# Softcap attention and a maxout MoE in one launch: left values in one pass, named score slots, larger weight loads, a new order of all work

## The chip, the cores and the metric

The kernel runs on one core of a Trainium2 chip. The core has a matrix engine (TensorE, PE in the profile, with its weight loads shown as PEld), VectorE (DVE), ScalarE (ACT), GpSimd (POOL) and SyncE (SP), each with its own list of instructions that it runs in order, and DMA queues that SP, ACT and POOL issue to. All matmuls here take bf16 operands and accumulate in float32 in PSUM. The metric is the device time of one launch in microseconds (us); a profile is of one execution, and its span is a little shorter than the time of that execution.

## The reference

```python
def _attn_ref(q, k, v, cap):                      # q, k, v: 8 x 12 x 448 x 64
    scale = 1.0 / np.sqrt(q.shape[-1])
    scores = scale * np.matmul(q, k.transpose(0, 1, 3, 2))
    scores = cap * np.tanh(scores / cap)          # cap = 30
    scores = scores - np.max(scores, axis=-1, keepdims=True)
    attn = np.exp(scores)
    attn = attn / (np.sum(attn, axis=-1, keepdims=True) + 1e-09)
    return np.matmul(attn, v)

def _moe_ref(x, w1, w2, w_out):                   # x: 3584 x 768
    g = np.maximum(x @ w1, x @ w2)                # w1, w2: 768 x 1024
    return g @ w_out                              # w_out: 1024 x 768

# x is the attention's output, (8, 448, 12 * 64) laid out as 3584 x 768
```

## The kernel before

**The algebra.** max(h1, h2) = relu(h1 - h2) + h2, so the kernel computes relu(x (w1 - w2)) w_out + x (w2 w_out). It makes w1 - w2 once (`subtract`, L377) and w2 w_out once (`turn_w2` L391 transposes w2, `premultiply` L406 multiplies, `keep_wm` L412 copies out). `stage1` is then x (w1 - w2) with a relu on the way out of PSUM (L627), `stage2` the two products summed in one PSUM bank, 6 + 8 matmuls, with a copy out (L660).

**The items.** The 96 heads are 24 items t of four heads, each item two pairs i = 2t + o. Keys stand in PSUM's rows, queries (448) in its columns. The 448 keys of a head are three blocks of 128 and a left block of 64. Per item:
- `scores` (L486): for each pair and each of three key blocks, two heads side by side as 64x128 tiles, into one slot of two banks; `tanh` (L491) on ACT empties it into the exps' tile. There are two such slots, taken in turn by scores, left scores and values alike.
- `left` (L499): the left 64 keys of all four heads, four 64x64 tiles at once; `tanh_left` (L503).
- `ex` (L507) and `ex_left` (L510): exp in place, on ACT; no maximum is subtracted, since tanh bounds the scores.
- `add` (L519) and `add_left` (L524) sum the exps of the key blocks on DVE, from item 3 on; `total` (L537, L541, L544) sums over the keys by a matmul with ones; `invert` (L549, L552, L555) takes 1/x on DVE.
- `values` (L569): 128x32 tiles, four heads abreast, three passes for the 128-key blocks, for each half u of the 64 value columns; then the left keys by one more pass of 128x32 (L573), in which half of the rows of the weights (`vl`) are zeros, since the left exps of two heads lie above each other. `fill_const` (L287, L288) writes the zeros once. `normalize` (L582) multiplies by 1/sum into `xT`, the x of the MoE, one DVE instruction per u.

**The MoE** works on groups: one PSUM bank, its matmuls and its way out. `Group.step` (L606) issues half a matmul (64 rows of the contraction, 64x128 tiles), and `M x y n` does n steps of two groups x and y, one in the upper and one in the lower half of the array; with -1 for one of them, half of the array is empty. Where x = y, step 2 issues full 128-row matmuls (L601); the last two groups run so. When a group moves from one half of the array to the other, `hand_over` (L615) puts a DVE nop between. Groups have one of four banks, `mm0` to `mm3`, which also serve totals and transposes.

**The loads.** `load` (L322, L329) and `load_v` (L347) bring q, k and v on POOL's queue, which casts to bf16. The first ten pairs (NX) are turned by PE (`transposes` L433, `keep_qkT` L441), later items by a DMA transpose on SP (`cross`, L453), which frees the raw tile `kqs`; k/q, v and the transposed tiles have two buffers each (KB, VB, QB). w2, w_out and w1 are loaded on POOL's queue too (L368, L359, L374): w1 and w2 in six blocks of 128 x 1024. Stores go out on SP (L637, L638, L642), those of the last tile on SP and ACT (L665 to L672). `keep_warm` (L449) issues filler matmuls early on.

**The order.** All of this is in one list of steps, ORDER, written out in the kernel and executed once to issue instructions: S scores, T tanh, L and TL left scores, E and EL exp, A and B adds, Y the total, V values, N normalize, O opens a group, M steps groups, H hands over, ev evicts, st stores, lk, lq, lv, lw1, lw2, lwo loads, cr a DMA transpose, X and XC a transpose by PE and its copy, W, P, OP, PC the premultiply, D fillers. Each engine runs its part of the list in that order and waits where data or a buffer is not there. MoE steps of the batches that are done fill PE between the attention steps of the next items; after item 23's values, PE has only MoE work. An excerpt, with item 4's values:

```python
M 10 8 3; L 5; Y 4 0; TL 5; V 4 0; Y1 4; V 4 1; E 10 0 3; Y2 4; Y3 4; S 11 0; M 10 9 1; lv 6 0; N 4 0;
M 10 9 2; M 8 9 1; N 4 1; M 8 9 1; lv 6 1; M 8 9 2; H 10; M 8 9 1; S 11 1; lv 6 2; T 11 0; A 5 0 1; M 8 9 3;
```

Of the kernel before, what the change touches and what calls it, by code (L numbers as in the profile page):

```python
# [9 lines left out]
ld0 k; ld0 q; ms0; lk 1 0; dm; ms; D 3 34; lw2 1; id; lq 1 0; lk 2 0; lw2 2;  # L10
cd k; cd q; lq 2 0; Xh 0 0 0; lwo 0 0; Xh 0 1; XCh 0 0; lw2 0; XCh 0 1;
lwo 0 1; S 0 0; lq 3 0; S 0 1; lq 4 0; T 0 0; lk 3 0; D 3 4; S 0 2; X 1 1; T 0 1; XC 1; D 3 6;
lv 0 0; W 2 2; T 0 2; W 1 3; lv 0 1; WC 2; L 0; E 0 0 3; S 1 0; WC 1; X 2 0; XC 2; D 3 8;
lv 0 2; OP 2 0 1; P 2 0 3; TL 0; P 2 0 1; OP 1 0 2; P 1 0 3; T 1 0; P 1 0 1; S 1 1; lv 0 3; W 0 3; EL 0; S 1 2;
WC 0; T 1 1; OP 0 0 0; P 0 0 2; T 1 2; P 0 0 1; S 2 0; lk 4 0; P 0 0 1; P 1 0 1; E 1 0 2; P 1 0 1; lw1 0;
S 2 1; P 1 0 2; P 2 0 1; lwo 1 0; P 2 0 1; PC 1 0; P 2 0 2; T 2 0; P 0 0 1; lk 5 0; PC 2 0; X 3 3; lw2 3;
E 1 2 3; P 0 0 1; XC 3; S 2 2; lwo 1 1; P 0 0 2; T 2 1; PC 0 0; lq 5 0; T 2 2; X 4 2; lq 6 0; L 1; lv 1 0;
XC 4; Y 0 1; TL 1; lv 1 1; sub 0 0; V 0 0; E 2 0 3; V 0 1; Y1 0; S 3 0; Y2 0; Y3 0; lv 1 2; OP 0 1 3; P 0 1 1;
T 3 0; N 0 0; P 0 1 3; lv 1 3; N 0 1; OP 2 1 0; P 2 1 2; EL 1; P 2 1 2; S 3 1; S 3 2; T 3 1; OP 1 1 2; P 1 1 2;
lw2 4; W 3 1; P 1 1 1; T 3 2; P 1 1 1; WC 3; S 4 0; E 3 0 2; S 4 1; OP 3 1 1; P 3 1 4; lw2 5; P 0 1 3; T 4 0;  # L20
P 0 1 1; P 1 1 1; lv 2 0; P 1 1 1; PC 0 1; P 1 1 2; E 3 2 3; P 2 1 1; lv 2 1; PC 1 1; S 4 2; X 5 3; lv 2 2;
T 4 1; P 2 1 1; XC 5; P 2 1 1; lv 2 3; P 2 1 1; T 4 2; OP 3 0 2; P 3 0 2; PC 2 1; lw1 4; L 2; Y 1 3; lk 6 0;
TL 2; V 1 0; lk 7 0; Y1 1; E 4 0 3; V 1 1; Y2 1; Y3 1; S 5 0; lq 7 0; N 1 0; W 5 0; lw1 2; W 4 3; N 1 1; T 5 0;
P 3 0 1; WC 5; P 3 0 1; lw1 5; S 5 1; EL 2; P 3 0 1; lw1 1; WC 4; S 5 2; P 3 0 1; lq 8 0; T 5 1; P 3 0 2;
P 3 1 2; PC 3 0; P 3 1 1; T 5 2; lk 8 0; P 3 1 1; OP 4 0 0; P 4 0 1; sub 4 0; P 4 0 3; lk 9 0; E 5 0 2; X 6 3;
PC 3 1; lq 9 0; P 4 0 2; XC 6; P 4 0 2; lw1 3; X 7 2; PC 4 0; S 6 0; XC 7; S 6 1; T 6 0; OP 5 0 1; P 5 0 2;
lv 3 0; sub 2 0; P 5 0 3; E 5 2 3; P 5 0 1; S 6 2; P 5 0 2; T 6 1; OP 4 1 3; P 4 1 1; lv 3 1; sub 5 0; P 4 1 4;
T 6 2; P 4 1 2; L 3; PC 5 0; Y 2 0; lv 3 2; TL 3; V 2 0; sub 1 1; Y1 2; E 6 0 3; V 2 1; Y2 2; Y3 2; S 7 0;
N 2 0; X 8 2; lv 3 3; N 2 1; X 9 1; T 7 0; lq 10 0; XC 8; P 4 1 1; EL 3; S 7 1; XC 9; S 7 2; lq 11 0; OP 5 1 0;
P 5 1 2; PC 4 1; P 5 1 1; T 7 1; P 5 1 1; A 3 0 1; P 5 1 2; lk 10 0; P 5 1 2; T 7 2; sub 3 0; O 0 2; M 0 -1 1;  # L30
lk 10 1; S 8 0; M 0 -1 1; E 7 0 2; M 0 -1 1; S 8 1; PC 5 1; lk 11 0; M 0 -1 2; A 3 0 2; M 0 -1 1; O 1 1;
M 1 -1 1; lk 11 1; M 1 -1 1; H 0; M 1 -1 1; T 8 0; M 1 0 1; A 3 1 1; M 1 0 1; lv 4 0; M 1 0 1; O 2 3; M 2 0 1;
B 3 0; M 2 0 1; E 7 2 3; lv 4 1; S 8 2; M 2 0 1; H 1; B 3 1; M 2 1 1; lv 4 2; M 2 1 1; T 8 1; M 2 1 1; ev 0;
O 3 0; M 3 1 1; lv 4 3; M 3 1 2; T 8 2; H 2; A 3 1 2; M 3 2 2; lk 12 0; cr 5; M 3 2 1; ev 1; O 4 2; M 4 2 1;
L 4; lk 12 1; M 4 2 1; TL 4; Y 3 1; V 3 0; lq 12 0; Y1 3; E 8 0 3; V 3 1; Y2 3; lk 13 0; Y3 3; S 9 0; M 4 2 1;
lv 5 0; N 3 0; M 4 3 2; N 3 1; M 4 3 1; lv 5 1; O 5 1; M 5 3 2; T 9 0; H 4; M 5 3 1; ev 2; lv 5 2; S 9 1;
M 5 4 1; ev 3; M 5 4 1; EL 4; M 5 4 1; lv 5 3; S 9 2; A 4 0 1; O 6 3; M 6 4 2; lk 13 1; M 6 4 1; T 9 1; H 5;
A 4 0 2; M 6 5 3; lq 13 0; ev 4; O 7 0; M 7 5 1; T 9 2; M 7 5 1; S 10 0; H 6; M 7 5 1; M 7 6 1; E 9 0 2;
lk 14 0; M 7 6 1; ev 5; S 10 1; M 7 6 1; O 8 2; M 8 6 1; lk 14 1; M 8 6 1; H 7; M 8 6 1; M 8 7 2; ev 6;
lq 14 0; T 10 0; M 8 7 1; O 9 1; M 9 7 1; A 4 1 1; M 9 7 2; E 9 2 3; lk 15 0; H 8; S 10 2; ev 7; M 9 8 3; cr 6;  # L40
B 4 0; lk 15 1; M 9 8 1; T 10 1; M 9 8 2; B 4 1; M 9 8 2; lq 15 0; T 10 2; M 9 8 2; A 4 1 2; M 9 8 1; O 10 3;
M 10 8 3; L 5; Y 4 0; TL 5; V 4 0; Y1 4; V 4 1; E 10 0 3; Y2 4; Y3 4; S 11 0; M 10 9 1; lv 6 0; N 4 0;
M 10 9 2; M 8 9 1; N 4 1; M 8 9 1; lv 6 1; M 8 9 2; H 10; M 8 9 1; S 11 1; lv 6 2; T 11 0; A 5 0 1; M 8 9 3;
lv 6 3; O 11 0; M 11 9 1; A 5 0 2; EL 5; M 11 9 1; S 11 2; M 11 9 1; lk 16 0; ev 8; M 11 10 2; T 11 1;
M 11 10 1; ev 9; M 11 10 1; cr 7; M 11 10 1; lk 16 1; M 11 10 2; T 11 2; M 11 10 1; S 12 0; lq 16 0; M 11 10 1;
# [12 lines left out]
M 20 18 2; L 7; lq 20 0; ev 18; Y 6 1; TL 7; V 6 0; Y1 6; lk 21 0; V 6 1; E 14 0 3; Y2 6; Y3 6; lk 21 1;
S 15 0; M 20 19 1; N 6 0; M 20 19 1; lv 8 0; M 20 19 1; N 6 1; O 21 0; M 21 19 2; lv 8 1; M 21 19 1; H 20;
S 15 1; T 15 0; ev 19; M 21 20 1; lv 8 2; M 21 20 2; A 7 0 1; O 22 1; M 22 20 1; EL 7; M 22 20 1; lv 8 3;  # L60
S 15 2; H 21; A 7 0 2; M 22 20 1; M 22 21 1; lq 21 0; M 22 21 1; T 15 1; ev 20; M 22 21 1; O 23 3; M 23 21 1;
cr 9; M 23 21 1; H 22; M 23 21 1; T 15 2; M 23 22 1; S 16 0; ev 21; M 23 22 3; E 15 0 2; M 23 22 1; S 16 1;
M 23 22 6; O 24 2; M 24 22 1; T 16 0; M 24 22 1; H 23; A 7 1 1; M 24 22 1; M 24 23 3; H 22 2; E 15 2 3; B 7 0;
M 22 23 1; S 16 2; M 22 23 1; H 24; M 22 23 1; B 7 1; M 22 23 1; T 16 1; M 22 23 2; lk 22 0; M 22 23 1;
A 7 1 2; M 22 23 1; O 25 0; M 25 23 1; T 16 2; M 25 23 1; ev 22; M 25 23 1; lk 22 1; L 8; ev 23; M 25 24 1;
TL 8; lq 22 0; Y 7 1; V 7 0; Y1 7; st 1 3; E 16 0 3; lk 23 0; V 7 1; Y2 7; Y3 7; lk 23 1; S 17 0; M 25 24 1;
N 7 0; M 25 24 2; lv 9 0; M 25 24 1; N 7 1; M 25 24 3; lv 9 1; T 17 0; M 25 24 1; A 8 0 1; S 17 1; M 25 24 2;
lv 9 2; O 26 3; M 26 24 1; A 8 0 2; EL 8; M 26 24 1; S 17 2; M 26 24 1; lv 9 3; H 25; M 26 25 2; T 17 1;
H 24 2; M 26 25 1; lq 23 0; M 24 25 1; cr 10; M 24 25 1; H 26; M 24 25 2; T 17 2; M 24 25 1; S 18 0; M 24 25 2;
E 17 0 2; M 24 25 1; S 18 1; O 27 1; M 27 25 1; ev 24; M 27 25 2; M 27 26 2; ev 25; M 27 26 3; T 18 0;  # L70
M 27 26 1; A 8 1 1; M 27 26 3; st 1 4; M 27 26 1; B 8 0; E 17 2 3; M 27 26 1; S 18 2; O 28 2; M 28 26 1; H 27;
B 8 1; M 28 26 2; T 18 1; M 28 27 2; H 26 2; A 8 1 2; M 28 27 1; M 26 27 2; T 18 2; M 26 27 2; lk 24 0; L 9;
# [132 lines left out]
def kernel(  # L205
# [11 lines left out]
    nc = tc.nc  # L217
# [13 lines left out]
    NQ = N // 2  # L231
    NJ = 3
    NX = 10
    KB = 2
    VB = 2
    QB = 2
    NS = 3
    W2T = 4
    WOP = 2
    R7 = S // 64  # L240
    OB = 4
# [502 lines left out]
```

## Time and profile before

| | us |
|---|---|
| median of 3 runs (lowest to highest) | 338.81 (338.31 to 342.69) |
| profiled execution | 338.55 |
| its span | 336.8 |
| PE busy | 325.7 (97%) |
| PEld busy | 194.3 |
| ACT busy | 275.6 (82%) |
| DVE busy | 229.2 (68%) |
| POOL busy | 169.6 (50%) |
| DMA moved | 45.90 MB, mean 136 GB/s |
| TensorE's mean granted clock | 0.989 |

Busy time is the union of an engine's instructions. In a group's line stand the code line, engine, operation, destination and source with their shapes, the count, the busy time and the mean of one instruction, then the idle time of the engine ahead of it and who ended it. Matmuls overlap in the array, so the mean of one is longer than the distance between two starts; distances are read from the timeline. A waits line names the engine and line that waited, what released it, the total, how often, and the longest.

### The profile page before, as it was taken

The numbers are of one execution on the slowest core, as the hardware profiler recorded it, in microseconds if no ns is written. First come the engines' busy times: TensorE is split into PE (matmuls) and PEld (weight loads), VectorE is DVE, ScalarE is ACT, GpSimd is POOL, SyncE is SP. The second block draws the span as 40 slices with busy tenths as digits, with TensorE's granted clock in tenths as the row PEclk, the third lists the DMA queues.
The fourth block names the chain that finished last, engine by engine and source line by source line (L and its number), as shares of the span: only waits on it lengthen the run. The fifth ranks groups of instructions, "written<-read, shape, count | busy, mean of one in ns | idle before, by whom it ended". The sixth has DMA issues, their size and how long they took to land.

```text
span 336.8 us, 9657 instructions
## 1 busy us (share of the span) xinstructions
PE 325.7 (97%) x4068; PEld 194.3 (58%) x4068; DVE 229.2 (68%) x410; ACT 275.6 (82%) x268; POOL 169.6 (50%) x250
## 2 busy tenths in 40 slices
PE   6999999999999999999999999999999999999994
PEld 5644556555767555555665564556565555567662
DVE  2355789786796658868778668866976778675321
ACT  4799989999989998998899998899899999910000
POOL 7475759966743872771783463677648202000000
PEclk9599999999999999999999999999999999999999
DMA  8999999999999999999999999999999953023033
GB/s 142 189 187 170 211 263 78 156 124 188 144 138 134 134 157 199 107 98 148 171 141 123 129 137 190 128 138 179 177 140 124 192 133 47 2 64 79 2 95 93
DMA packets 136108, 45.90 MB, mean 136 GB/s; under 512 B 116352, under 2 KB 131072, under 8 KB 136064
## 3 DMA queue, kind: packets, MB, share of 16 engines
q0 software_dynamic: 96320, 25.08, 78.2%
q1 hardware_dynamic: 39440, 19.86, 33.6%
q8 instruction: 32, 0.52, 0.7%
q10 hardware_dynamic: 304, 0.33, 0.3%
q14 instruction: 12, 0.10, 0.1%
HBM read 47.45 MB, written 11.01 MB: 174 GB/s over the span
## 4 chain that ended last, share of the span: by engine, by line
PE 79%; DVE 8%; ACT 5%; DMA 4%; issue 2%; POOL 1%; DVEq 0%; POOLq 0%
PE mm L606 52%; PE s L486 8%; PE s L569 6%; PE mm L406 4%; ACT e L507 3%; PE s L499 2%; DMA gT<-in_moe_w_dram 2%; PE mm L544 2%; PE s L573 2%; DMA out_dram<-osb 2%; ACT e L491 1%; DVE xT L582 1%; DVE esum L524 1%; PE mm L433 1%; PE mm L391 1%
## 5 line engine op out<-in xcount | busy, mean ns | idle before, releaser
L491 ACT ACTIVATE e<-s 128x896 bf16<-128x896 f32 x144 | 127.4, 928 | 2.9 <-PE s L486 2.9
L507 ACT ACTIVATE e<-e 128x2688 bf16<-128x2688 bf16 (+2 forms) x72 | 122.8, 1707 | 0.0
L606 PE MATMUL mm<-wo_sb,gT 64*128 64x384 bf16 x864 | 114.5, 323 | 0.0
L606 PE MATMUL mm<-wm_sb,xT 64*128 64x384 bf16 x648 | 101.0, 323 | 0.0
L606 PE MATMUL mm<-xT,wd_sb 64*128 64x448 bf16 x768 | 99.1, 350 | 0.6 <-DVE gT L627 0.4
L329 POOL DMA_DIRECT2D kqs<-in_k_dram x76 | 54.2, 716 | 70.0 <-DMA qkT<-kqs 69.7
L606 PEld LDWEIGHTS <-gT 64*128 64x128 bf16 x864 | 59.1, 94 | 25.1 <-DVEq L615 0.2
L606 PEld LDWEIGHTS <-wd_sb 64*128 64x128 bf16 x768 | 52.1, 94 | 24.6 <-issue 2.6
L606 PEld LDWEIGHTS <-xT 64*128 64x128 bf16 x648 | 50.4, 94 | 18.6 <-issue 0.6
L486 PE MATMUL s<-qkT 64*128 64x448 bf16 x288 | 55.6, 355 | 3.3 <-ACT e L491 1.2
L627 DVE TENSOR_SCALAR gT<-mm 128x448 bf16<-128x448 f32 x64 | 39.5, 622 | 13.3 <-PE mm L606 12.9
L660 DVE COPY osb<-mm 128x384 f32<-128x384 f32 x54 | 29.4, 555 | 25.7 <-PE mm L606 25.0
L347 POOL DMA_DIRECT2D vp<-in_v_dram x48 | 30.4, 638 | 22.3 <-PE mm L606 10.5
L519 DVE TENSOR_TENSOR esum<-e 128x896 bf16<-128x896 bf16 x42 | 26.1, 621 | 22.8 <-ACT e L507 18.1
L329 POOL DMA_DIRECT2D kqs<-in_q_dram x38 | 35.4, 931 | 2.4 <-issue 2.4
L569 PE MATMUL s<-e,vp 128*32 128x448 bf16 x576 | 35.8, 352 | 0.0
L486 PEld LDWEIGHTS <-qkT 64*128 64x128 bf16 x288 | 17.0, 94 | 28.5 <-issue 14.4
L503 ACT ACTIVATE el<-s 128x896 bf16<-128x896 f32 x24 | 22.0, 917 | 13.3 <-PE s L499 12.7
L347 POOL DMA_DIRECT2D vl<-in_v_dram x48 | 29.3, 619 | 6.6 <-DMA wo_sb<-in_moe_w_out_dram 4.1
L670 ACT COPY osb<-mm 128x192 f32<-128x192 f32 x1 | 0.3, 318 | 36.8 <-DMA out_dram<-osb 36.8
L582 DVE TENSOR_TENSOR xT<-s,inv 128x448 bf16<-128x448 f32 x48 | 27.8, 620 | 2.6
L519 DVE TENSOR_TENSOR esum<-esum,e 128x896 bf16<-128x896 bf16 x42 | 26.2, 624 | 2.2 <-PE mm L606 0.3
(57 smaller groups left out, 269.9 us busy)
## 6 DMA issues: line engine op xcount, KB each, us to landing
out_dram<-osb SPq DMA_DIRECT2D x54, 192.0 KB, 4.9
vp<-in_v_dram POOLq DMA_DIRECT2D x38, 160.0 KB, 6.9
kqs<-in_q_dram POOLq DMA_DIRECT2D x47, 112.0 KB, 6.3
kqs<-in_k_dram POOLq DMA_DIRECT2D x76, 56.0 KB, 4.4
osb<-in_moe_w_dram POOLq DMA_DIRECT2D x4, 512.0 KB, 7.5
gT<-in_moe_w_dram POOLq DMA_DIRECT2D x6, 256.0 KB, 6.2
wo_sb<-in_moe_w_out_dram POOLq DMA_DIRECT2D x4, 384.0 KB, 9.0
xT<-in_moe_w_dram POOLq DMA_DIRECT2D x2, 512.0 KB, 7.2
```

The costliest lines, as they stand in the source:

```text
L329: nc.gpsimd.dma_start(out=to, in_=x)
L347: nc.gpsimd.dma_start(out=to, in_=x)
L486: nc.tensor.matmul(s[:, h, :S], k_of(t, o, h, j), q_of(t, o, h))
L491: nc.scalar.activation(expo[i][:, 2 * j : 2 * j + 2, :], slots[i, j][:, :, :S], AF.Tanh, scale=scale / cap)
L503: nc.scalar.activation(left_e[t], slots[t][:, :, :S], AF.Tanh, scale=scale / cap)
L507: nc.scalar.activation(e, e, AF.Exp, scale=float(cap))
L519: nc.vector.tensor_add(d, e[:, 0:2, :] if j == 1 else d, e[:, 2 * j : 2 * j + 2, :])
L569: nc.tensor.matmul(ps[r, u, :S], vp[t % VB][:, m, j if turned_by_pe(t) else 2 * j, u::2], expo[2 * t + o][:, 2 * j + h, :], start=(j == 0) ...
L582: nc.vector.tensor_mul(x, vals[t][:, u, :S], sums[t, 3])
L606: ins = nc.tensor.matmul(self.ps, w[r], x[r], start=first, stop=self.at == [self.n, self.n]).ins
L627: nc.vector.tensor_relu(gT[b // 2][:, f, cs], ps)
L660: nc.vector.tensor_copy(o[:, hs], ps)
```

## The change

- The left scores (`left`) are eight matmuls of 64x32 tiles per item in place of four of 64x64.
- The left values get a step of their own, VL (`values_left`), ahead of the other values: eight matmuls of 64 rows x 32 columns, both halves u in one pass, without zeros in `vl`. For u = 1 the heads stand in swapped order, so `normalize` is two instructions of 64 partitions there.
- The left exps live behind the exps of the item's second pair, and are exponentiated with them: per item one exp of 2688 and two of 1792 elements, no separate one for the left.
- Score slots have names s0 and s1, and each S, L and VL says which it takes.
- w1 and w2 come in three blocks of 128 x 2048 (8 KB rows) instead of six of 1024, each with two rows of the matrix per partition; all subtracts are on DVE.
- The premultiply is made of groups (0 to 11) like the MoE's, in 64-row halves; the last two groups of the MoE are paired too. Groups 12 and up are those that were 0 and up.
- KB, VB, QB are 3, W2T is 6. The output tiles are one fixed tile of four slots, and w1's last block has a tile of its own.
- 34 filler matmuls in place of 52, and ORDER is new as a whole: loads come in bunches between the other steps, and the exps, scores and MoE steps of neighbouring items are mixed in another order.

`NCUT` is 0, so the parts of the new code that split an item's queries do nothing.

```diff
-    KB = 2
-    VB = 2
-    QB = 2
+    KB = 3
+    VB = 3
+    QB = 3
...
-    W2T = 4
+    W2T = 6
...
-    s_psum = ctx.enter_context(tc.tile_pool(name="s_psum", bufs=2, space=PSUM))
+    s_psum = ctx.enter_context(tc.tile_pool(name="s_psum", bufs=1, space=PSUM))
...
-        eng.memset(vl[i][64:, 0::3, :], 0.0)
-        eng.memset(vl[i][:64, 1:3, :], 0.0)
...
-    def load_w2(c):
-        nc.gpsimd.dma_start(out=w2b[:, c, :], in_=x_rows(moe_w2, c))
+    def load_w2(c):
+        nc.gpsimd.dma_start(out=w2b[:, 2 * c : 2 * c + 2, :], in_=block_of(moe_w2, c))
...
+    def s_tile(z):
+        return s_psum.tile([P, 2, 512], f32, name=f"s{z}", bufs=1)
...
-        s = slots[t] = s_psum.tile([P, 2, 512], f32, name="s")
+        ps = slots[n, "l"] = s_tile(z)
         for o in range(2):
             for h in range(2):
-                r = slice(64 * (h ^ o), 64 * (h ^ o) + 64)
-                nc.tensor.matmul(s[r, o, :S], k_of(t, o, h, NJ), q_of(t, o, h))
+                for g in range(2):
+                    r = 64 * (h ^ o) + 32 * g
+                    nc.tensor.matmul(
+                        ps[r : r + 32, o, :w], k_of(t, o, h, NJ)[:, 32 * g : 32 * g + 32], q_of(n, o, h)
+                    )
...
+    def values_left(n, z):
+        t, c0, w = ITEMS[n]
+        ps = vals[n] = s_tile(z)
+        for m in range(4):
+            for u in range(2):
+                x = m ^ (2 * u)
+                o, h = heads(t)[x]
+                a = slice(64 * (h ^ o), 64 * (h ^ o) + 64)
+                nc.tensor.matmul(
+                    ps[R32[m], u, :w], vl[t % VB][a, x, u::2], left_of(n)[a, o, :], start=True, stop=False
+                )
...
-        for m, ((o, h), r) in H:
-            nc.tensor.matmul(ps[r, u, :S], vl[t % VB][:, m, u::2], left_e[t][:, o, :], start=False, stop=True)
...
-        nc.vector.tensor_mul(x, vals[t][:, u, :S], sums[t, 3])
+        if u == 0:
+            nc.vector.tensor_mul(x, vals[n][:, 0, :w], sums[n, 3][:, :w])
+            return
+        for a in range(2):
+            r, to = slice(64 * a, 64 * a + 64), slice(64 - 64 * a, 128 - 64 * a)
+            nc.vector.tensor_mul(x[to], vals[n][r, 1, :w], sums[n, 3][to, :w])
...
-ORDER: V 4 0; Y1 4; V 4 1; E 10 0 3; Y2 4; Y3 4; S 11 0; M 10 9 1; lv 6 0; N 4 0;
+ORDER: M 22 20 5; lk 15 1; lk 12 0; lk 12 1; lv 4 2; lk 14 1; VL 4 0; lv 4 0; V 4 0;
+ORDER: lv 5 0; lv 6 3; lq 13 0; lq 15 0; lk 17 1; lq 14 0; A 4 1 2; B 4 0; H 24; B 4 1; Y 4 0; Yi 4 1; Yi 4 2; Yi 4 3; N 4 0;
+ORDER: V 4 1; S 5 5 1; T 5 5; E 5 0 0 3; M 22 20 6; H 22; M 24 20 2; cr 6; S 6 1 1; T 6 1; N 4 1; M 24 20 1; ev 20;
```

More of the change, by code (lines that the diff above doesn't have):

```diff
@@ L383, in mm_tile, with keep_warm @@
         return newest[bank]
+    def keep_warm(bank, n):
+        if newest.get(bank) is None or newest[bank] is not warmed.get(bank):
+            warmed[bank] = mm_tile(bank)
+        for _ in range(n):
+            nc.tensor.matmul(warmed[bank][:, :P], warm, warm, start=True, stop=True)
     w2T = {}
@@ L475, in heads @@
         return [divmod(m, 2) if turned_by_pe(t) else divmod(m, 2)[::-1] for m in range(4)]
-    expo = {}
-    left_e = {}
-    slots = {}
-    def scores(i, j):
-        t, o = divmod(i, 2)
-        s = slots[i, j] = s_psum.tile([P, 2, 512], f32, name="s")
-        for h in range(2):
-            nc.tensor.matmul(s[:, h, :S], k_of(t, o, h, j), q_of(t, o, h))
-    def tanh(i, j):
-        if j == 0:
-            expo[i] = att.tile([P, 2 * NJ, S], bf16, name=f"e{i % 2}")
-        nc.scalar.activation(expo[i][:, 2 * j : 2 * j + 2, :], slots[i, j][:, :, :S], AF.Tanh, scale=scale / cap)
@@ L493, in left, with cut, exps_of @@
-    def left(t):
-        s = slots[t] = s_psum.tile([P, 2, 512], f32, name="s")
+    ITEMS = [(t, 0, CUT) for t in range(NCUT)] + [(t, CUT, S - CUT) for t in range(NCUT)]
+    ITEMS += [(t, 0, S) for t in range(NCUT, N // 2)]
+    def cut(n):
+        return ITEMS[n][2] < S
+    exps = {}
+    slots = {}
+    def exps_of(n, o):
+        key = (n, 1 if cut(n) else o)
+        if key not in exps:
+            if key[1]:
+                exps[key] = att.tile([P, 8 * S], bf16, name="e1")
+            else:
+                exps[key] = att.tile([P, 6 * S], bf16, name="e0")
+        return exps[key]
@@ new lines, in e_of, with left_of, scores @@
+    def e_of(n, o, h, j):
+        w = ITEMS[n][2]
+        if cut(n):
+            x = 4 * (o if j < 2 else 2) + 2 * h + (j if j < 2 else o)
+        else:
+            x = 2 * j + h
+        return exps_of(n, o)[:, x * w : (x + 1) * w]
+    def left_of(n):
+        w = ITEMS[n][2]
+        b = 12 if cut(n) else 6
+        return exps_of(n, 1)[:, b * w : (b + 2) * w].rearrange("p (o s) -> p o s", o=2)
+    def s_tile(z):
+        return s_psum.tile([P, 2, 512], f32, name=f"s{z}", bufs=1)
+    def scores(n, s, z):
+        t, c0, w = ITEMS[n]
+        ps = slots[n, s] = s_tile(z)
+        if cut(n):
+            parts = [(s, 0), (s, 1)] if s < 2 else [(0, 2), (1, 2)]
+        else:
+            parts = [divmod(s, NJ)]
+        for x, (o, j) in enumerate(parts):
+            for h in range(2):
+                nc.tensor.matmul(ps[:, h, x * w : (x + 1) * w], k_of(t, o, h, j), q_of(n, o, h))
@@ new lines, in tanh_left, with ex, add @@
+    def tanh_left(n):
+        w = ITEMS[n][2]
+        nc.scalar.activation(left_of(n), slots[n, "l"][:, :, :w], AF.Tanh, scale=scale / cap)
+    def ex(n, o, j0, j1):
+        w = ITEMS[n][2]
+        m = (4 if cut(n) else 2) * w
+        e = exps_of(n, o)
+        hi = j1 * m if j1 <= NJ else NJ * m + 2 * w
+        nc.scalar.activation(e[:, j0 * m : hi], e[:, j0 * m : hi], AF.Exp, scale=float(cap))
+    esum = {}
+    def add(n, ab, j):
+        w = ITEMS[n][2]
+        if n not in esum:
+            esum[n] = att.tile([P, 4, S], bf16, name="esum")
+        d = esum[n][:, 2 * ab : 2 * ab + 2, :]
+        e = exps_of(n, ab)[:, : 6 * S].rearrange("p (b s) -> p b s", s=S)
@@ L546, in invert @@
-    def invert(t, step):
+                for (o, h), r in HR:
+                    nc.tensor.matmul(ss[r, :w], ones[:, :32], e_of(n, o, h, j), start=(j == 0), stop=False)
+            for (o, h), r in HR:
+                nc.tensor.matmul(ss[r, :w], ones2[:, h ^ o, :32], left_of(n)[:, o, :], start=False, stop=True)
+        else:
+            for (o, h), r in HR:
+                nc.tensor.matmul(ss[r, :w], ones[:, :32], esum[n][:, 2 * o + h, :], start=True, stop=True)
+    def invert(n, step):
+        w = ITEMS[n][2]
+        b = w // 32
@@ L656, in done @@
             if (b, t) not in osbs:
[L657 removed]
+                osbs[b, t] = osb_all[:, (7 * (b // 2) + t) % OB, :DM]
             o = osbs[b, t]
```

559 lines of the change are left out of this document (251 added, 308 removed).

## The prediction

> **What bounds the kernel now.** I read the page from its head: engines, slices, chain, and then windows, groups, waits and the timeline.
>
> ```profile
> span 336.8 us, 9657 instructions
> ...
> PE 325.7 (97%) x4068; PEld 194.3 (58%) x4068; DVE 229.2 (68%) x410; ACT 275.6 (82%) x268; POOL 169.6 (50%) x250
> ...
> ACT  4799989999989998998899998899899999910000
> ...
> PEclk9599999999999999999999999999999999999999
> ...
> PE 79%; DVE 8%; ACT 5%; DMA 4%; issue 2%; POOL 1%; DVEq 0%; POOLq 0%
> ```
>
> PE is the bound: 97% of the span and 79% of the chain. ACT is nearly as full until slice 35 and empty after it, and the third line of slices that I show has one weak place, slice 2, where TensorE was granted about half its clock. The windows, cut at the half clock, at the values of items 0 and 2, at the values of item 23 and at the last matmul, say where PE is not full:
>
> ```profile
> 9.20:16.10 6.90, 6.18 (x69) 4.45 (x68) 2.54 (x4) 5.46 (x5) 3.01 (x6) 0.53 1.23 193
> ...
> 48.30:297.70 249.40, 247.37 (x3114) 145.88 (x3106) 190.29 (x337) 235.25 (x228) 141.02 (x197) 1.00 1.27 137
> 297.70:332.10 34.40, 34.34 (x380) 22.50 (x379) 13.42 (x25) 0.00 (x0) 0.00 (x0) 1.00 0.24 62
> 332.10:336.80 4.70, 0.00 (x0) 0.00 (x0) 0.34 (x1) 0.32 (x1) 0.00 (x0) 0.97 0.26 63
> ```
>
> (Columns: window, its length, busy time of PE, PEld, DVE, ACT, POOL, then clock, DMA share and GB/s.) So the time has four parts: a start that waits for loads, 249 us in which PE is full and ACT 94% full, 34 us of PE alone, and 4.7 us of stores. A busy PE still hides gaps between starts. Counting starts against the steady spacing (below), PE lost 9.0 us before item 0's values, 1.1 more until 48.3, 9.7 in the long window and about 1 after it.
>
> **Work on PE.** The timeline of one item gives the prices:
>
> ```profile
> 155.42 0.38 PE L499 MATMUL s<-qkT 64*64 64x448 bf16 x4
> 155.73 0.37 PE L544 MATMUL mm<-esum,ones 128*32 128x448 bf16 x4
> 155.93 0.74 PE L569 MATMUL s<-e,vp 128*32 128x448 bf16 x12
> 156.50 0.36 PE L573 MATMUL s<-el,vl 128*32 128x448 bf16 x4
> 156.69 0.74 PE L569 MATMUL s<-e,vp 128*32 128x448 bf16 x12
> 157.25 0.36 PE L573 MATMUL s<-el,vl 128*32 128x448 bf16 x4
> 157.55 0.36 PE L486 MATMUL s<-qkT 64*128 64x448 bf16 x2
> ```
>
> Three passes of L569 take 0.57, one of L573 0.19: a 448-column pass costs 0.19 us whatever is packed beside it. From L499 to L544 there are 0.31, from L573 to L486 0.30: a change of tile shape costs about 0.10 to 0.12 on top of the pass.
> - Left values: two L573 passes per item become one of eight 64x32 tiles. 24 x 0.19 = **-4.6**. The trace has no eight-tile pass. The four tiles of L499 start within 10 ns, 3 to 4 ns apart; four further starts would add 16 ns to this pass and to that of the left scores: 48 x 0.016 = 0.8, or nothing. I take +0.4.
> - Changes of tile shape along PE's list rise from 126 to 143 (the 64x32 pass is a shape of its own, although some 64x128 blocks were joined): 17 x 0.10 = **+1.7** (1.9 at the shown 0.11).
> - A step that feeds one of two paired groups leaves half the array empty. There were 18, there are 36. A pair of 384-column matmuls starts every 0.162 us, so each lone one wastes 0.081: **+1.5**.
> - w2 w_out in 64-row pairs: 96 full matmuls become 96 pairs. L601's full matmuls, 14 in 2.29 us (327.32 to 329.61), also cost 0.163. Nothing either way; the same for the last two groups.
> - 18 fewer fillers (L449, 0.056 each at full clock): 1.0 less work, but it stood in waits, so it counts nothing.
>
> Sum: -4.6 + 0.4 + 1.7 + 1.5 = **-1.0**, between -1.6 and -0.2.
>
> **The start.** w2's blocks were 0.5 MB; the chain waits on the first to 10.49:
>
> ```profile
> 3.86 6.63 DMA gT<-in_moe_w_dram
> 10.54 1.89 PE mm L391 x16
> ```
>
> Now the queue holds v, q and k loads ahead and blocks of 1 MB. At the row of 1.97 us for 0.5 MB and 0.57 for a k or q load, the first w2 block lands at 8.6 to 10.4 and the second part of item 0's v at 20 to 23, so item 0's values come at 21 to 23.5 (24.6 before). But less of PE's list lies ahead of them (11.3 against 15.5 us, by the prices above), so PE has lost 9.7 to 12.2 there instead of 9.0, hardly more until item 2: +0.7 to +3.2. I take the lower half, **+1.5**, since the three k/q/v buffers let the loads of items 1 and 2 be issued without waiting for a transpose.
>
> **The long middle.** The waits view:
>
> ```profile
> POOL kqs L329 <- DMA qkT<-kqs: 69.7, 15, 7.2
> ...
> PEld L486 <- DVE xT L582: 7.7, 22, 0.8
> ```
>
> (total us, times, longest.) PE's 9.7 us of gaps are: scores waiting for ACT to empty a slot 1.8, scores waiting for normalize (L582) to empty one 1.8 (most of the 7.7 is a weight load ahead of time), groups opening on a bank that DVE empties 1.8, hand-overs 0.5, and some 3.8 in pieces under 0.1.
> - ACT: its list has 24 instructions fewer. The exps of the left scores (L510, 0.95 us) go into exps of 1792 or 2688 elements: before 2436 + 1713 + 973 + 950 = 6.07 us per item, now 2436 + 2 x 1713 = 5.86, so -5.0 by mean durations; by the spacing of starts on ACT (2.33, 1.583, 0.84 and 0.84 us) -2.3. I take -2.3, off PE's path. Counted from the start, ACT's list is also some 3 us shorter against PE's at item 2. Scores then wait less: -1.3.
> - DVE: normalize of the swapped half is two instructions of 64 partitions. L524 takes 617 ns on 64 partitions and L519 621 on 128, of 896 columns both, so halving the partitions saves nothing: each half costs L582's 620 ns, 24 x 0.62 = +14.9 us. With one subtract (1.22) from POOL and one copy from ACT, DVE rises to some 245 us, 73% of the span. The work itself is hidden behind PE, but it stands in line ahead of the evictions and frees the values' slot 0.62 us later. That would hold back a next score in the 15 places that wait now: 0 to 15 x 0.62 = +9.3; I take +0.6, since the order has scores into the other, named slot in between.
> - Openings, hand-overs and pieces: 132 hand-overs as before, but in the new order evictions stand several steps ahead of the opening that needs their bank, and of the 6.1 us I take -3.5 (0 to -5.4), somewhat over half.
>
> Together **-4.2**; bounds -7.2, and +9.3 if every such place is exposed and nothing else gains, which would come out like the second rival.
>
> **The load queue** is where POOL gets its gates. The 76 k loads wait 69.7 us for the DMA transposes (L453) that free their buffer, 15 waits of 4.6 us, and still v is there 14 to 18 us ahead of its use. With three buffers the gate is an item earlier, but loads now come in bunches, and a v load can sit behind a k load that waits. With issue times of 0.72 (k), 0.93 (q) and 0.63 (v) and the landings of this trace, v at items 10, 12, 13 and 20 is only 1 to 6 us ahead. I count **nothing**, hidden under the MoE matmuls; uncovered it is the second rival.
>
> **The end.** Before, the last matmul ends at 332.04 with one half tile to evict, and 3.4 us later its stores have landed. Now the last pair ends two groups at once and a third waits: on DVE 0.56 + 0.56 + 0.36, on SP six issues of 0.55 (two took 1.10 at 328.01), the last landing 2.1 after its issue. That gives 6.85 from last matmul to end instead of 4.74: **+2.1** (0 to +3).
>
> **Sum** against the profiled run (span 336.8, 1.75 outside it, 338.55; the median of the runs shown is 338.81): -1.0 + 1.5 - 4.2 + 2.1 = -1.6. **Forecast 337.0**, 333 to 341, no change that a measurement of this kernel can tell (about 2%, 332.0 to 345.6).
>
> **Rivals.**
> - Everything hides. The gaps of the middle fall from 9.7 to 2.5 (2.5 of the small pieces stay), the start costs its lower end and the end 1.5 (middle of its bounds): -1.6 + 0.7 - 7.2 + 1.5 = -6.6, **332**, spread 330 to 334. For it: ACT's 3 us of lead; against it: two slots in PSUM still couple PE to ACT, and ACT has 94% of the window.
> - Slower: the load queue is late. A transpose lands 4 us (alone) to 11 us after its issue, median 7.9; DMA share is already 1.27. If the mean landing in a bunch is at 10 or above, a gated k load holds the v loads behind it past their slack, at four places, by 2 to 3 us each, and PE's list stops there since it is in order: about +9, **345.5** (343 to 348). It decides when k loads take over 0.75 us and q loads over 1.6 in the queue. For it: the bunches; against it: most other v loads are 7 to 26 us ahead.
> - The half clock lasts. It was granted from 9.2 to 16.1, where PE had 69 matmuls, some of them fillers. If thinner work keeps it to 19.5 to 22.9, the matmuls there lose 1.7 to 3.4: **339.6**.
> - The left values do not run eight abreast, and the change does not do what its words say: 24 x 0.19 back, **341.6**. L499 has tiles of different rows writing one bank in 3 ns steps, which speaks against it.
>
> The Trainium skill bears on the last two. "TensorE: Matmul & The Clock Gate" (Part 1) says that the clock halves after an idle window of about 3.4 us and comes back after a busy one; the half clock here lasted 6.9 us, which is two such windows, and one more would be the third rival's price. "TensorEngine Tiling (Array Packing)" (Gotcha 1) says that different row tiles cannot access one PSUM bank at the same time, which would give the fourth; the row of L499 does not agree.
>
> **Chances.** Forecast 0.42, all hides 0.27, load queue 0.18, half clock 0.08, not abreast 0.05. Faster by over 2%: some two thirds of the second case and a little of the first, 0.20. Slower: nearly all of the load queue, a little of the first and last, 0.18. Within: 0.62. The range reaches from the second case's low end into the third's: 330 to 347.
>
> **What would show it.** One pass of 64x32 tiles in about 0.2 us ahead of each item's values; ACT busy 270 or less; DVE about 245; gaps of 5 to 6 us in PE's middle; 6.9 us after the last matmul. PE's weight loads waiting on vp or vl DMAs for more than a microsecond would show the queue late; a PEclk below 9 past slice 2, the clock. The prediction is wrong if the scores wait for ACT or for normalize longer than now, since the new order decides that and I could only bound it.

## The result, and the profile after

The changed kernel takes 367.8 us (median of 4 runs, 367.0 to 368.0) against 338.6 before: 1.083 times as long, 95% interval 1.074 to 1.092. The forecast was 337.0 with a range of 330 to 347. The profiled execution took 368.0, its span is 366.2. The page of the changed kernel, with the lines that answer to those shown of before:

```profile
span 366.2 us, 9971 instructions
...
PE 333.6 (91%) x4270; PEld 199.9 (55%) x4270; DVE 246.2 (67%) x432; ACT 278.5 (76%) x243; POOL 166.2 (45%) x243
...
PEclk8589999989999999999999999998999879999997
...
PE 68%; DVE 14%; ACT 5%; DMA 5%; POOL 3%; issue 3%; SPq 0%; DVEq 0%; ACTq 0%; POOLq 0%
```

PE fell from 97% of the span to 91%, and its share of the chain from 79% to 68%; DVE's share rose from 8% to 14%. Between the start and the last slice the clock row has an 8 or a 7 in three places, where before it had none. The windows of the changed kernel, cut at its own half clock, at the values of items 0 and 2, at those of item 23 and at its last matmul (columns as before):

```profile
7.20:20.90 13.70, 10.69 (x139) 6.46 (x139) 3.85 (x7) 11.77 (x11) 7.30 (x14) 0.50 1.22 203
...
50.00:326.90 276.90, 258.27 (x3214) 151.71 (x3214) 204.43 (x357) 236.85 (x207) 134.73 (x188) 0.98 1.00 120
326.90:359.20 32.30, 32.22 (x381) 22.79 (x373) 12.48 (x22) 0.00 (x0) 0.00 (x0) 1.00 0.14 38
359.20:366.20 7.00, 0.00 (x0) 0.00 (x0) 1.38 (x3) 0.32 (x1) 0.00 (x0) 0.71 0.57 169
```

The start takes little longer than before (item 2's values come at 50.0 instead of 48.3), the stretch of PE alone is 2.1 us shorter (32.3 instead of 34.4), the end is 2.3 us longer, and the middle has grown from 249.4 to 276.9 us; PE stands idle for 18.6 us of it, before for 2.0. The waits view names the two largest pieces (L538 is the line of the values, L553 normalize of the first half):

```profile
PE s L538 <- DVE xT L553: 13.5, 8, 2.4
...
PE s L538 <- DMA vp<-in_v_dram: 3.6, 1, 3.6
```

Neither wait is in the waits view of before, where no value waited for DVE. The timeline of PE around one of the eight, and that of DVE beside it:

```profile
74.41 0.75 PE L538 MATMUL s<-e,vp 128*32 128x448 bf16 x12
74.99 0.57 PE L501 MATMUL mm<-esum,ones 128*32 128x448 bf16 x4
77.92 0.75 PE L538 MATMUL s<-e,vp 128*32 128x448 bf16 x12 [2.36 <-DVE xT L553]
```

```profile
75.60 0.65 DVE L508 STREAM_TRANSPOSE st<-mm 128x448 f32<-128x448 f32 x1 [0.47 <-PE mm L501]
76.29 0.24 DVE L511 RECIPROCAL rs<-st 128x14 f32<-128x14 f32 x1
76.56 0.65 DVE L514 STREAM_TRANSPOSE inv<-rs 128x448 f32<-128x448 f32 x1
77.24 0.62 DVE L553 TENSOR_TENSOR xT<-s,inv 128x448 bf16<-128x448 f32 x1
```

PE computes the first half of the values, then the total, and then does nothing until DVE has made 1/sum and normalized the first half; 0.06 us later the second half starts. It needs nothing of that. In ORDER, items 1, 4, 5, 8, 9, 15, 17 and 20 have `N n 0` directly ahead of `V n 1`. Both halves are one PSUM tile of two banks; the second half writes into a tile that an earlier step of the list reads, so it is made to wait for that reader, though the reader's bank is another one. By idle time the eight waits are the 13.5 us of the view; from start to start, less the usual distance, they are 15.4, since the matmuls ahead of a wait still show as busy for part of it. In the kernel before, `V t 1` stands ahead of `N t 0` for every item.

### The profile page after: what moved, and what is told of

It reads as the page before. It is cut to its first block, busy times and chain, and to the rows that moved or that the text cites. A ratio compares the mean times of both kernels' runs of the same rounds, so it can differ in the third digit from the quotient of the medians.

```text
span 366.2 us, 9971 instructions
## 1 busy us (share of the span) xinstructions
PE 333.6 (91%) x4270; PEld 199.9 (55%) x4270; DVE 246.2 (67%) x432; ACT 278.5 (76%) x243; POOL 166.2 (45%) x243
## 3 DMA queue, kind: packets, MB, share of 16 engines
q1 hardware_dynamic: 39440, 19.86, 24.1%
## 4 chain that ended last, share of the span: by engine, by line
PE 68%; DVE 14%; ACT 5%; DMA 5%; POOL 3%; issue 3%; SPq 0%; DVEq 0%; ACTq 0%; POOLq 0%
PE mm L581 46%; PE s L437 7%; PE s L538 7%; DVE esum L483 3%; ACT e L468 2%; DVE esum L478 2%; DVE xT L553 2%; DMA vp<-in_v_dram 2%; ACT e L446 2%; DMA gT<-in_moe_w_dram 2%; PE mm L365 2%; PE mm L501 2%; PE s L455 2%; POOL kqs L282 1%; DVE osb L644 1%
## 5 line engine op out<-in xcount | busy, mean ns | idle before, releaser
L468 ACT ACTIVATE e<-e 128x1792 bf16<-128x1792 bf16 (+1 forms) x72 | 139.8, 1950 | 0.9
L581 PE MATMUL mm<-wo_sb,gT 64*128 64x384 bf16 x896 | 121.5, 330 | 0.0
L581 PE MATMUL mm<-xT,wd_sb 64*128 64x448 bf16 x768 | 95.8, 351 | 0.1
L581 PEld LDWEIGHTS <-gT 64*128 64x128 bf16 x896 | 62.6, 96 | 26.7 <-issue 3.9
L300 POOL DMA_DIRECT2D vp<-in_v_dram x48 | 30.8, 645 | 67.8 <-PE s L437 48.3
L581 PEld LDWEIGHTS <-xT 64*128 64x128 bf16 x672 | 50.3, 95 | 20.5 <-issue 3.1
L538 PE MATMUL s<-e,vp 128*32 128x448 bf16 x576 | 34.8, 363 | 17.0 <-DVE xT L553 13.5
L612 DVE TENSOR_SCALAR gT<-mm 128x448 bf16<-128x448 f32 x64 | 38.2, 620 | 11.5 <-PE mm L581 10.1
L557 DVE TENSOR_TENSOR xT<-s,inv 64x448 bf16<-64x448 f32 x48 | 29.9, 622 | 9.8 <-PE s L538 5.7
L538 PEld LDWEIGHTS <-vp 128*32 128x32 bf16 x576 | 16.1, 97 | 28.1 <-issue 22.1
L483 DVE TENSOR_TENSOR esum<-esum,e 64x896 bf16<-64x896 bf16 x42 | 26.0, 619 | 7.0 <-ACT e L468 5.6
L437 PEld LDWEIGHTS <-qkT 64*128 64x128 bf16 x288 | 18.5, 95 | 22.4 <-issue 10.8
```

Of the source, the lines that this page charges most:

```text
L300: nc.gpsimd.dma_start(out=to, in_=x)
L437: nc.tensor.matmul(ps[:, h, x * w : (x + 1) * w], k_of(t, o, h, j), q_of(n, o, h))
L468: nc.scalar.activation(e[:, j0 * m : hi], e[:, j0 * m : hi], AF.Exp, scale=float(cap))
L483: nc.vector.tensor_add(d, d, left_of(n)[r])
L538: nc.tensor.matmul(vals[n][R32[m], u, :w], vp[t % VB][:, x, j if turned_by_pe(t) else 2 * j, u::2], e_of(n, o, h, j), start=False, stop=(j ...
L557: nc.vector.tensor_mul(x[to], vals[n][r, 1, :w], sums[n, 3][to, :w])
```

## The experiments

All edits are given against the kernel named. The kernel before took 338.1 to 338.4 us beside them.

**The order of normalize and values.** In the changed kernel, eight neighbours change places:

```diff
-N 4 0; V 4 1;
+V 4 1; N 4 0;
```
(and so for items 1, 5, 8, 9, 15, 17 and 20)

> The changed kernel with one edit: for items 1, 4, 5, 8, 9, 15, 17 and 20, whose list has normalize of the first half (N n 0) ahead of the values of the second half (V n 1), the two neighbours change places. Theory A (an order between steps that no data needs: both halves are one PSUM tile, so the later values wait until DVE has read the first half, and all of PE's list with them): the eight stalls of the second half, 15.4 us in the profile, go, and with them the half clock that follows the two longest (3.4 us each, half of it lost): 368 - 15.4 - 3.4 = 349 (347 to 351). Rival B (DVE is late because normalize is now three instructions, and PE waits for DVE wherever it is put): the waits come back as scores or totals waiting for DVE, 360 or more. Rival C (the load queue is the cause): no change, 365 or more.

348.9 us, ratio 1.035 (1.027 to 1.042). Eight exchanged neighbours are worth 18.9 us. No value waits for DVE any more, and the page has the clock whole until the last slice:

```profile
PE 328.8 (95%) x4270; PEld 195.0 (56%) x4270; DVE 245.7 (71%) x432; ACT 277.6 (80%) x243; POOL 166.1 (48%) x243
...
PEclk9999999999999999999999999999999999999998
```

The eight waits summed to 15.4 us in the trace, from start to start. Of the other 3.5, 1.3 is the wait for a DMA at item 20, which shrank from 3.6 to 2.3. The 2.2 that are left were not taken apart; the three stretches of half clock past the start, 13.7 us in all, went as well and are the likely place. Theory A has its number; rivals B and C, as causes of this part, fall.

**The same order put into the kernel before**, which needs no added work:

```diff
-V 4 0; Y1 4; V 4 1; E 10 0 3; Y2 4; Y3 4; S 11 0; M 10 9 1; lv 6 0; N 4 0;
+V 4 0; Y1 4; Y2 4; Y3 4; N 4 0; V 4 1; E 10 0 3; S 11 0; M 10 9 1; lv 6 0;
```
(and so for the same seven other items)

> The kernel before the change, with the order of theory A put into it alone: for the same eight items the reciprocal and the normalize of the first half stand ahead of the values of the second half; nothing else differs, no instruction is added. Theory A: each of the eight second halves waits for transpose, reciprocal, transpose and normalize on DVE (0.65 + 0.24 + 0.65 + 0.62), of which some 0.4 are over: 8 x 1.8 = 14, so about 353 (349 to 357). Rival B (the DVE work that was added makes the wait): no work was added here, so 339 to 341.

352.8 us, ratio 1.044 (1.038 to 1.050), 14.3 more than before. The waits view of this run has the line that the changed kernel has, eight times again:

```profile
PE s L558 <- DVE xT L571: 13.5, 8, 1.7
```

So the order alone makes a loss of this size, in either kernel.

**The load queue.** On top of the first edit, item 20's four v loads go ahead of item 22's first:

```diff
+lv 20 2; lv 20 3; lv 20 1; lv 20 0; lv 22 0; lk 45 1; lk 46 0;
-lv 22 0; lk 45 1; lk 46 0;
```
(and they are taken out of their old places, up to fifteen loads behind item 22's)

> The kernel of the run before this one, with the four v loads of item 20 moved ahead of the v load of item 22 that waits for item 19's values to free its buffer. Theory A with the queue as second cause: the 3.6 us in which item 20's values wait for a DMA go, and the half clock after them (6.8 us, half of it lost): 7 us less than that run, about 342 (340 to 345). If the half clock has another cause, 3.6 less, 345 to 346. If the loads of other items are pushed late in their turn, a new wait for a DMA of 2 us or more shows at item 21 or 22.

345.7 us, ratio 1.022 (1.020 to 1.025): 3.2 less, and no matmul of values waits for a DMA any more. What it removes is seen on POOL's timeline and in the chain of the changed kernel:

```profile
273.84 0.61 POOL L300 DMA_DIRECT2D vp<-in_v_dram  x1 [20.54 <-PE s L437]
```

```profile
284.29 7.00 DMA vp<-in_v_dram
...
291.43 1.34 PE s L538 x12
```

POOL stood for 20.5 us at item 22's v load, which waits until item 19's values have left its buffer (the view names the score right behind them), and item 20's loads, whose buffer was free, stood behind it. The gain is the wait itself (3.6 in the changed kernel, 2.3 after the first edit) and little more, not the 7 expected: after the first edit there was no half clock at that wait any more.

**The start.** On top of that, 32 filler matmuls more between 7 and 19 us:

```diff
+D 3 6; S 0 2 0; ... D 3 10; W 1 1; ... D 3 8; S 0 3 1; ... D 0 4; S 0 5 1; ... D 0 4; S 1 0 0;
```

> The kernel of the run before this one, with 32 more filler matmuls in five places between 7 and 19 us, where PE waits for ACT and for loads. If the missing fillers kept the clock at half (13.7 us after 7.2, against 6.8 us before the change): half clock 6.8 us or less, the values of item 0 come 1.5 to 3.4 us earlier, time 3 us less than that run, about 339. If the loads set the start: no more than 0.5 us less, whatever the clock.

345.6 us. The half clock that the run without them had from 9.1 to 19.4 is gone in the profile, and the time is the same within 0.2. That the fillers brought the clock back is not shown: the profile of the first edit has it whole here too, without them. But the half clock costs this start nothing that the time shows. Item 0's values come at 23.1 with these fillers, at 23.3 with half clock, and at 23.8 in the first edit's profile with neither.

**What is left, 7.3 us.** On the kernel of the load queue, the left values go back to two passes and normalize to one instruction per half:

```diff
-        for m in range(4):
-            for u in range(2):
-                x = m ^ (2 * u)
+        for u in range(2):
+            for m in range(4):
+                x = m
...
-        if u == 0:
-            nc.vector.tensor_mul(x, vals[n][:, 0, :w], sums[n, 3][:, :w])
-            return
-        for a in range(2):
-            r, to = slice(64 * a, 64 * a + 64), slice(64 - 64 * a, 128 - 64 * a)
-            nc.vector.tensor_mul(x[to], vals[n][r, 1, :w], sums[n, 3][to, :w])
+        nc.vector.tensor_mul(x, vals[n][:, u, :w], sums[n, 3][:, :w])
```

> The changed kernel with both moves made so far (normalize behind the values for eight items, item 20's loads first), with the left values of both halves in the same tiles, so in two passes, heads not swapped, and normalize of the second half as one instruction again: PE 24 x 0.19 = +4.6, DVE 24 x 0.62 = -14.9. If what is left of the loss (346 against 338) comes from DVE's added work: 343 or less in spite of the pass. If the added DVE work is hidden: 346 + 4.6 = 350 (349 to 351).

342.5 us, ratio 1.013 (1.010 to 1.017), the first of the two expected values: with one pass per item more on PE it is 3.2 faster, so the 14.9 us on DVE had cost at least 3.2, and 7.8 if the passes cost their full price of 4.6. Between item 2's values and item 23's PE is busy for 252.1 us without this edit and with it, and idle for 3.5 and 0.5. So the net of 3.2 is measured and the split is not. Of the 4.2 us that remain to the kernel before, 2.3 lie behind the last matmul. The changes of tile shape (17 more, 1.7 by their price) and the lone MoE steps (18 more, 1.5) would more than make up the rest, which no run took apart.

**The left values alone, in the kernel before.** Left scores and left values as in the change, order and loads as before:

```diff
-L 5; Y 4 0; TL 5; V 4 0; Y1 4; V 4 1;
+L 5; VL 4; Y 4 0; TL 5; V 4 0; Y1 4; V 4 1;
```
(with `left`, `values_left`, `values` and `normalize` of the change)

> The kernel before the change with one part of the change alone: left scores as 64x32 tiles, left values as one pass of eight 64x32 tiles (right behind the next item's left scores, which have the same shape, so that no change of shape is added), heads swapped for the second half, normalize of that half as two instructions, no zeros. Order, buffers and loads as before. Theory A (this part is sound, the new order lost the time): 24 passes of 0.19 less, some 0.4 back for the later starts: -4.2, so 334.3 (333 to 336.5). Rival B (the DVE work that it adds, 14.9 us, holds back scores and evictions): the gain is eaten, 337.5 or more.

353.7 us, ratio 1.046 (1.043 to 1.049): no gain but a loss of 15. Its waits view, however, names DVE for 0.9 us only, and ACT for most:

```profile
PE s L475 <- ACT e L480: 19.2, 23, 1.1
```

The second score after the values waits for a tanh: the pool gave it the slot of the first score, not that of the values. At seven of the twenty items from 3 to 22 it even starts before normalize has emptied the values' slot. So slots of one name are not strictly taken in turn, and this run mixes two things. In the kernel before, one score of the twenty waits so, and starts 0.9 us later than the others.

**Its own shape.** The same with `VL 4` directly ahead of `V 4 0`:

> The run before this one with the left values directly ahead of the other values, so that their shape stands alone between two passes of 128x32: two changes of shape more per item, 24 x 2 x 0.10 = 4.8, at most 24 x 2 x 0.12 = 5.8. Theory A (a one-pass step costs two changes of shape if nothing of its shape stands beside it, which eats the gain): 4.5 to 6 us above the run before this one, about 339. If a change of shape were hidden by the weight loads: no more than 1 us above it.

353.7 us again. In the trace the pass of left values now starts 0.29 us behind the total and the values 0.31 behind it, where a pass takes 0.19: two changes of shape, 0.10 and 0.12, some 5.4 us over 24 items, as priced. The waits for the tanh are shorter by as much (13.7 instead of 19.2). PE's work was not what set the time in this kernel, so this run could not show its price in the time.

**Named slots.** To take the slots' choice out, `s0` and `s1` are used strictly in turn, first in the kernel before:

```diff
-        s = slots[i, j] = s_psum.tile([P, 2, 512], f32, name="s")
+        s = slots[i, j] = s_tile()          # and so for left scores and values
...
+    taken = []
+
+    def s_tile():
+        taken.append(0)
+        return s_psum.tile([P, 2, 512], f32, name=f"s{len(taken) % 2}", bufs=1)
```

> The kernel before the change with one edit: the two score slots have names and are taken strictly in turn, instead of two buffers of one name, of which the pool gives the one that it holds to be free first. In the run with the left values alone, the program of the second score after the values waits for the tanh of the first score (same slot) and not for normalize; in the kernel before this holds for some items only. If the slots are the price: 336 to 338 (up to 2 us less, those waits); if not, 338 to 339.

336.8 us, ratio 0.9955 (0.9938 to 0.9973): a small gain, clear of one, and the only part of the change that paid when tried alone. With the left values:

> The run with the left values alone, with the slots named and taken in turn. Theory D (the 15 us of that run came from the slot that the pool chose, about 1.1 us of waiting for a tanh per item, not from DVE's added work): 334 to 337. Rival B (normalize, 0.62 longer, frees the values' slot later and ACT has no slack, 24 x 0.62 = 15): 349 to 354.

358.1 us, ratio 1.058 (1.055 to 1.061). Theory D falls, and the loss is larger than rival B had it. And normalize of the second half in two instructions, with nothing else:

```diff
-        nc.vector.tensor_mul(x, vals[t][:, u, :S], sums[t, 3])
+        if u == 0:
+            nc.vector.tensor_mul(x, vals[t][:, 0, :S], sums[t, 3])
+            return
+        for a in range(2):
+            r = slice(64 * a, 64 * a + 64)
+            nc.vector.tensor_mul(x[r], vals[t][r, 1, :S], sums[t, 3][r, :])
```

> The kernel before with named slots, and normalize of the second half as two instructions of 64 partitions without anything else of the change (no swap of heads, left values as before): DVE +14.9, nothing else. Rival B: 349 to 354. Theory D: within 3 us of the named slots alone.

351.3 us, ratio 1.039 (1.036 to 1.041): 14.5 more than the named slots alone, for 14.9 us of DVE work. Here one microsecond on DVE costs one microsecond, although DVE is 70% busy. The window from 48 to 298 us, of the named slots alone and of this run:

```profile
48.00:298.00 250.00, 248.71 (x3140) 146.30 (x3134) 191.78 (x340) 234.90 (x227) 139.63 (x196) 1.00 1.20 135
```

```profile
48.00:298.00 250.00, 237.55 (x2974) 141.23 (x2967) 195.85 (x341) 227.13 (x220) 140.47 (x196) 1.00 1.21 135
```

In the same stretch PE is busy 11 us less and ACT 8. The waits view says for what; the named slots alone first, then this run, then the run with left values and named slots:

```profile
PE s L492 <- DVE xT L588: 0.4, 2, 0.2
```

```profile
PE s L492 <- DVE xT L593: 12.5, 22, 0.9
```

```profile
PE s L481 <- DVE xT L591: 24.1, 23, 1.3
```

Once per item a score waits for normalize to give back the values' slot. A chain runs from the total over five or six DVE instructions to that score, and PE's values run beside it. With the named slots alone the score starts 0.06 us after normalize ends, 3.35 after the total, at nearly every item from 3 to 22; with the second normalize split it starts 3.99 after the total. The 0.63 more, 24 times, is 15.1, against the 14.5 measured.

The wait grows by half a microsecond per item more when the left values are added, and the time by 0.28. One item of each run, on PE and on DVE, first with the split normalize alone and then with left values:

```profile
160.72 0.39 PE L505 MATMUL s<-qkT 64*64 64x448 bf16 x4
161.04 0.37 PE L550 MATMUL mm<-esum,ones 128*32 128x448 bf16 x4
...
165.02 0.36 PE L492 MATMUL s<-qkT 64*128 64x448 bf16 x2 [0.58 <-DVE xT L593]
...
163.17 0.62 DVE L589 TENSOR_TENSOR xT<-s,inv 128x448 bf16<-128x448 f32 x1
163.71 1.25 DVE L593 TENSOR_TENSOR xT<-s,inv 64x448 bf16<-64x448 f32 x2
```

```profile
154.06 0.39 PE L495 MATMUL s<-qkT 64*32 64x448 bf16 x8
154.26 0.38 PE L564 MATMUL s<-el,vl 64*32 64x448 bf16 x8
154.57 0.37 PE L540 MATMUL mm<-esum,ones 128*32 128x448 bf16 x4
...
158.66 0.36 PE L481 MATMUL s<-qkT 64*128 64x448 bf16 x2 [0.99 <-DVE xT L591]
...
156.71 0.63 DVE L587 TENSOR_TENSOR xT<-s,inv 128x448 bf16<-128x448 f32 x1
157.35 1.26 DVE L591 TENSOR_TENSOR xT<-s,inv 64x448 bf16<-64x448 f32 x2
```

The left values were two of the eight passes beside the chain; now they are one pass ahead of its start, so the total comes 0.51 after the left scores instead of 0.32. They have the left scores' shape, and no change of shape is added here. The chain itself is 0.10 longer (4.09 instead of 3.99 from total to score): with the heads swapped, the second half's normalize starts 0.64 after the first's, when that has ended, and without the swap 0.54. 24 x 0.29 = 7.0, against the 6.8 measured between the two runs. The passes taken from beside the chain saved nothing: the first score comes 1.44 after the total instead of 1.82, but the second, which waits, does not come sooner.

**Shortening the chain.** Both halves normalized by one instruction, at the place of the second half's, and then at that of the first half's:

```diff
-        x = xT[b // 2][:, 2 * q + u, (b % 2) * S : (b % 2 + 1) * S]
-        nc.vector.tensor_mul(x, vals[t][:, u, :S], sums[t, 3])
+        if u == 0:                          # then: u == 1
+            return
+        x = xT[b // 2][:, 2 * q : 2 * q + 2, (b % 2) * S : (b % 2 + 1) * S]
+        inv = sums[t, 3].rearrange("p (a s) -> p a s", a=1).to_broadcast([P, 2, S])
+        nc.vector.tensor_mul(x, vals[t][:, :, :S], inv)
```

> The kernel before with named slots, and normalize of both halves as one instruction of 896 columns: a fixed part of some 0.15 us less per item on DVE and on the release of the values' slot, 24 x 0.15 = 3.6. Rival B (that release is on the path): 334 to 336. Theory D: 337 to 338.5.

> The kernel before with named slots, and normalize of both halves as one instruction (1.09 us in the run before this one), now at the place in DVE's list where the first half's stood, ahead of the hand-over that waits for a matmul. The run before this one had it at the second half's place and was 2.5 us slower than the named slots alone. If that place was the price: 335.5 to 337, at or below the named slots alone, in which scores wait for normalize for only 0.8 us over all, so that there is little left to win. If the one instruction itself is the price: 339 again.

339.4 us (1.0035, 1.0018 to 1.0051) and 337.1 us (0.9955, 0.9938 to 0.9972). In the first, at five of the twenty items from 3 to 22 the instruction starts 0.4 to 0.6 us late, and the score after it too; it waits in DVE's list behind a hand-over, and its group names the MoE matmul in the last column:

```profile
L591 DVE TENSOR_TENSOR xT<-s,inv 128x896 bf16<-128x896 f32 x24 | 26.2, 1092 | 5.2 <-PE mm L615 3.2
```

At the early place it costs nothing, but it wins nothing over the named slots either: with those the chain was just short enough. Longer by 0.62 costs the whole 0.62 per item. Shorter by 0.07 (1.09 instead of 1.16 for both halves) gains nothing: the score now starts 0.09 after normalize's end and only 0.03 sooner after the total, since PE's own work is then the bound.

## Why the prediction was wrong

**The step that failed** is the DVE line of the middle, "+0.6, since the order has scores into the other, named slot in between", and with it the sum "Together -4.2". It had two faults.

- It looked only for waits that the kernel before has. A wait that a new order adds must be looked for in the new order: which step now stands ahead of which, and whether both touch one tile. `N 4 0` ahead of `V 4 1` stood in the excerpt of the diff. It is 15.4 us of waiting and 3.5 that came with it, the 18.9 of the first experiment. No rival had this mechanism. The sign that the prediction gave for being wrong is not what showed: in the changed kernel scores wait about as long as before (1.5 us for normalize and 0.8 for a tanh, before 0.9 and 1.2), and it is the values that wait.
- It took DVE's added 14.9 us as hidden behind PE, with DVE at 73% of the span. The instructions lie in a chain (total, transpose, reciprocal, transpose, normalize, release of the slot, next score, tanh) that closed just in time at nearly every item. The bound that was written, 0 to 9.3, counted only the places that waited already; alone it cost 14.5 in the kernel before, with named slots, and at least 3.2 in the new order (the net of the run with two passes).

**The rivals.** The load queue happened, at one of the four places that were named (item 20, by way of item 22's gated load), for 3.2 us and not 9. The half clock at the start happened too (13.7 us in the profile, up to 20.9, inside the stated 19.5 to 22.9) and cost nothing that the time shows. That everything hides was wrong. The left values do run eight abreast: the group's row and the starts in the trace, eight within some 23 ns, and the next step's start mostly 0.314 us after the first, which is a pass of 0.19 and a change of shape of 0.12.

```profile
L528 PE MATMUL s<-e,vl 64*32 64x448 bf16 x192 | 9.2, 359 | 0.1
```

The Trainium skill's "TensorEngine Tiling (Array Packing)" (Gotcha 1) would have tiles of different rows kept out of one bank at once; this trace does not agree for its eight tiles, four of which share each bank.

**The other terms.** The end: 6.85 us from the last matmul to the end of the span were forecast, 7.0 came. A change of shape at 0.10 to 0.12: 0.10 into the new pass and 0.12 out of it. DVE at 245 us: 246.2. The start, at +1.5, was put too low: item 0's values were forecast for 21 to 23.5 and came at 24.1. With the 11.3 us of PE's list that the prediction counts ahead of them, 12.8 are lost there, 3.8 more than before, where 3.2 was the bound; item 2's values came 1.7 us later than before. The prices of a load behind that forecast, 1.97 and 0.57, are not those of the trace of before: the packets of one 0.5 MB block of w2 took 1.4 to 2.3 us, spread over the 16 engines, and those of a k or q load 0.7 to 0.9. The half clock of before, read as 9.2 to 16.1, ran from 8.8 to 15.7. ACT's exps did become shorter (58.8 + 81.3 us of instructions against 145.7), but that ACT would be busy for 270 or less was wrong: 278.5. PE's saved work, -1.0, is not seen in any run that carried it.

So the 29.4 us against the 338.4 beside the experiments are 18.9 for the order of normalize and values, 3.2 for item 20's loads, 3.2 net for left values and their normalize, 2.3 for the end, and 1.8 not taken apart.

## What to carry to other kernels

In a list of steps that is written out, a step inherits a wait from whichever step stands ahead of it and touches the same tile; after a reorder, go through the pairs that changed places and ask for each whether one now reads what the other writes, by tile and not by byte. An engine's busy share says little about work that stands in a chain between two full engines: ask how much later the last link comes, times how often. Before a pass is taken away, see what ran beside it; a pass that covered a chain saves nothing.

## What the runs showed of the hardware

In the changed kernel, two of the eight waits (before 77.92 and 248.23) lost 2.7 us each, 2.4 of them idle in the records, and each was followed by 3.4 us at half the granted clock; with the wait of 3.6 for a DMA the clock fell as well, for 6.8. Item 20's wait lies within that stretch. The other five, of 1.0 to 2.2, all eight of 1.9 in the second experiment and the wait of 2.3 that was left in the first had none after them. "TensorE: Matmul & The Clock Gate" of the Trainium skill (Part 1) has windows of about 3.4 us, and the lengths of these stretches agree with it. So do those at the start of all runs that have one: 3.4, 6.8, 10.2 or 13.7 us. Unexpected is that so short a wait of an engine that is otherwise full is followed by half clock, and so can cost more than itself. Whether the length alone decides, or also when the wait falls, these cases can't tell: in the run with the left values' own shape the clock fell at 10.9 within a wait of 2.1, and in the kernel before at 8.8 with no single idle piece above 1.2 us.
